# A fused state-space and MLP kernel with its whole order of operations replaced

## The chip, the cores and the metric

The kernel runs on one core of a Trainium2 chip. The metric is the device time in microseconds of one execution, the median of several runs.

## What is computed

A long convolution gated by two projections, and then a dense block, each behind a layer norm and with a residual; S = 2048 positions, D = 640 channels, F = 1728.

```python
x = A_q
h  = x + A(layernorm(x), A_k, A_v, shift_k, ssm_k, ssm_D)
h2 = h + B(layernorm(h), w1, b1, w2)

A(q, k, v): k_shift = sum over 4 taps of k shifted in time, times shift_k[:, tap]
            kv = k_shift * v
            y  = irfft(rfft(kv, 2S) * rfft(ssm_k, 2S))[:S] + kv * ssm_D
            return q * y
B(x):       h = x @ w1 + b1;  return (h * tanh(softplus(h))) @ w2
```

## The kernel before

Every piece of work is an operation with a name, the engines that may run it, and the operations it needs. A list written out in the source, `ORDER`, gives one total order of all operations. The emitting loop walks the list; every engine executes its own instructions in the order in which the list has them. A token may carry `@n`, which of the four PSUM pairs (1024 float32 columns per partition) the operation takes, and `:d`, `:a` or `:p`, which engine runs it if it is not the first that the operation allows. Loads and stores named `d_*`, the swaps `sw*` and the transposing copies `tr*` are issued by SyncE; three small loads, `d_dr`, `d_cst` and `d_sk`, are issued by ScalarE and stand in its instruction order between its other work.

The stages, with the names used below:

- **Constants.** `idn` and `kz` on GpSimd; `warm` loads ScalarE's table and runs one Mish; `wm` is nine matmuls on zeros on TensorE. `d_cst` loads the transform matrices that the s1 stages multiply with and a mask; `d_sk` loads the four taps per channel; `d_dr` loads the vector D.
- **The kernel of the convolution.** `d_n0` to `d_n4` load ssm_k; `dadd` adds D to its first sample; `k1pe` transposes it on TensorE, `k1ev` copies it out of PSUM; `s1kpe` / `s1kev` (20 groups) are the first step of the transform, `s2kpe` / `s2kev` (22 groups, with the tables `d_g0` to `d_g7`) the second. The swaps `sw` exchange its real and imaginary halves by DMA; they need every `s2kev`.
- **The taps.** `cfpe` is one matmul on the taps (it needs `d_cst` and `d_sk`), `coef` four copies on VectorE, and `wsh0` to `wsh3` spread them over a mask into tap matrices. The four `wsh` may run on GpSimd or VectorE; GpSimd is the first allowed.
- **k and v.** `d_k`, `d_v` load; `ktpe` transposes k on TensorE, `ktev` copies it out, `ktsh` copies a shifted row on GpSimd; `kspe` applies the tap matrices, `kv` multiplies with v on VectorE; `s1v` and `s2v` are the transform of kv.
- **Product and inverse.** `pr` (20 products on VectorE), `i1pe` / `i1ev` (20 groups), `i2pe`, `i2a`, `i2b` / `y` (16 tiles).
- **Norms and gate.** `d_x` loads q; `ln1`, `ln1p`, `lnx` are its layer norm on VectorE, GpSimd and ScalarE or GpSimd; `wb`, `h`, `bn`, `pow`, `hc` gate, add and normalise; `trpe` / `trev` or `tr` transpose the result.
- **The dense block.** `m1pe` multiplies with w1 (`d_w1`), `hb` applies Mish on ScalarE, `m2pe` multiplies with w2 (`d_w2a`, `d_w2b`, `d_w2c`; `w2z` zeroes two quarters), `res` adds the residual on VectorE, `d_out` stores. The 2048 rows are five units of 256, 256, 512, 512 and 512.

The copies out of PSUM go to ScalarE or VectorE, as the list says (`EV`). Helper lines: L264 is a copy on ScalarE, L266 on VectorE; L328 issues all plain loads of SyncE; L399 and L400 are the two halves of s1; L425 is stage 2, L453 a swap, L464 a product, L485 i1, L537 i2, L604 the first dense product, L669 and L677 the second.

Of the kernel before, what the change touches and what calls it, by code (L numbers as in the profile page):

```python
# [34 lines left out]
s2kev_108 s2kpe_72@3 kspe0_1@0 d_x1 s2kev_72 kv1_1 d_x0 s2kpe_66@2 s2kpe_102@3 s2kev_66 kv0_1 kspe4_1@1 s2kev_102 s2kpe_120@2 kv4_1 kspe3_1@0
s2kev_120 s2kpe_126@3 kv3_1 s2kpe_78@1 s2kev_126 s2kpe_0@2 s2kev_78 s2kpe_114@3 s2kev_0:d s2kpe_36@0 s2kev_114 s2kpe_54@1 s2kev_36:d s2kpe_84@2
s2kev_54 s2kpe_60@3 s2kev_84 ln1_0 kspe2_1@1 s2kev_60 s2kpe_48@0 kv2_1 ln1p0 s1vpe0_2@2 s2kev_48 s1vpe1_1@3 s1vev0_2:d s1vpe2_1@1 d_x2 s1vev1_1
s1vpe1_0@0 d_x3 s1vev2_1 s1vev1_0:d s1vpe4_3@2 s1vpe3_2@3 s1vev4_3 s1vpe0_0@1 s1vev3_2:d s1vpe2_2@0 s1vev0_0 s2kpe_90@2 s1vpe1_2@3 s1vev2_2 s2kev_90:d
s1vpe0_3@1 s1vev1_2 s1vpe1_3@0 s1vev0_3:d s1vpe0_1@2 s1vev1_3 s1vpe3_0@3 s1vev0_1:d s1vpe4_1@1 s1vev3_0 s2kpe_30@0 s1vev4_1:d s2v0pe_0@2 s2kev_30
s2v0pe_48@3 s2v0ev_0 ln1_1 sw1_0 s1vpe2_0@1 s2v0pe_64@0 sw1_1 s2v0ev_48 lnx0:p s1vev2_0:d s2v0pe_112@2 sw0_0 ln1p1 s2v0ev_64 sw4_0 s2v0pe_32@3  # L40
s2v0ev_112:d s2v0pe_80@1 sw3_1 s2v0ev_32 s1vpe3_1@0 lnx1:p sw0_1 ln1_2 s1vpe4_0@2 s2v0ev_80 sw3_0 s1vpe3_3@3 sw4_1 ln1_3 s1vev3_1 ln1p2 s1vpe2_3@1
sw2_0 s1vev4_0 s1vev3_3:d sw2_1 s1vpe4_2@0 lnx2:p s1vev4_2 s2v0pe_96@3 pr1_64 ln1p3 s2v0pe_16@2 s2v0ev_96 s2v2pe_32@0 s1vev2_3:d lnx3:p s2v0ev_16
s2v2pe_80@3 pr1_96 s2v2ev_32 s2v2pe_112@1 s2v2pe_64@2 s2v2ev_112 pr1_0 s2v2pe_48@0 s2v2ev_64 s2v2pe_0@1 pr0_96 s2v2ev_0 s2v2pe_16@2 pr1_32 s2v2ev_16
s2v1pe_96@1 pr0_64 s2v2ev_48 i1pe1_1@2 s2v2ev_80 s2v2pe_96@0 pr3_0 s2v1ev_96 i1pe1_2@3 pr3_32 i1ev1_1 s2v1pe_64@1 pr0_32 s2v2ev_96 s2v1pe_0@2 i1ev1_2
pr0_0 s2v1pe_32@0 s2v1ev_0 pr3_64 i1pe1_3@3 d_w14 s2v1ev_64 d_w10 i1pe0_2@2 pr3_96 d_w11 s2v1ev_32 d_w12 i1pe0_1@1 pr4_0 d_w13 i1ev1_3 d_t2m i1pe3_3@0
i1ev0_1 pr2_96 i1pe3_1@3 i1ev3_3 pr2_64 i1pe3_0@1 i1ev0_2 i1pe0_3@0 pr2_0 i1ev3_0 i1pe0_0@2 pr2_32 i1ev3_1 i1pe3_2@1 i1ev0_3 pr4_96 i1pe2_0@3 i1ev0_0
# [4 lines left out]
m1pe0_6@1 ln1_11 ln1p4 m1pe0_3@3 tr3 ln1p7 d_w2b ln1_13 h5 y8 lnx4:p m1pe0_2@0 hb0_6 ln1_9 ln1p8 wb4 lnx7:p hb0_3 wb7 lnx6 m1pe0_0@2 wb6 bn5 hb0_2 h4
hb0_0 h6 lnx8:p m1pe0_5@1 h7 ln1p15 ln1p11 m1pe1_1@3 bn4 m1pe1_4@0 lnx11:p pow5 wb8 hb0_5 m1pe1_2@2 ln1p9 hb1_1 m1pe1_0@1 hb1_4 wb11 bn7 hb1_2 hb1_0
ln1_14 ln1p10 m1pe1_5@3 m1pe1_3@0 hc5 m1pe1_6@2 i2pe9@1 hb1_5 hb1_3 pow7 bn6 i2pe14@3 pow6 h8 pow4 hc7 tr5 hb1_6 lnx15:p y9 m2pe0@0 bn8 y14 hc6
m2pe1@2 pow8 wb15 tr7 lnx9 hc4 wb9 ln1_12 lnx10 m2pe3@1 tr6 ln1p12 tr4 m2pe2@3 wb10 res3 res0 ln1p14 h11 h9 lnx14 res1 lnx12 bn9 h10 hc8 bn10 ln1p13
bn11 lnx13:p m1pe2_6@1 pow10 wb13 wb14 m1pe2_2@0 pow11 h13 hb2_2 hc10 wb12 h14 pow9 hc9 hc11 tr8 bn13 h12 bn14 m1pe2_3@2 tr10 hb2_6 m1pe2_4@0
m1pe2_0@1 d_out0 res2 bn12 pow13 h15 hb2_3 m1pe2_5@2 tr11 tr9 hb2_4 bn15 pow12 m1pe2_1@0 m1pe3_5@3 hb2_5 pow15 m1pe3_3@2 d_out1 hc13 hb2_0 m1pe3_2@1
hb3_5 hc15 hb3_2 m1pe3_0@3 pow14 tr13 hb3_0 m1pe3_6@1 hc12 hb3_6 hc14 m1pe3_1@3 m1pe3_4@1 hb2_1 hb3_4 d_out3 tr15 tr12 m2pe5@0 hb3_1 m2pe7@1 tr14
m2pe4@3 res7 res5 m2pe6@1 m1pe4_2@0 res4 m1pe4_5@3 res6 hb4_2 m1pe4_4@1 d_out2 d_out7 hb4_4 m1pe4_1@0 hb4_5 m1pe4_6@1 hb3_3 m1pe4_3@3 hb4_1 m2pe9@2
# [681 lines left out]
```

## Time and profile before

| | |
|---|---|
| median of 3 runs | 222.97 us (222.88 to 223.0) |
| the profiled execution | 223.02 us |
| its span, first to last instruction | 221.2 us |
| TensorE, matmul | 212.5 us busy |
| VectorE | 137.6 us |
| ScalarE | 127.9 us |
| GpSimd | 62.0 us |
| DMA | 30.98 MB moved |

All times inside the profile count from the first instruction. The 1.8 us between the span and the execution's time lie around it. A matmul's end is modelled, so TensorE's busy time is no measure of its load by itself. In the list of instructions a bracket gives the idle time of the engine just before, and what ended it; in a row of a stretch the columns are start and end, length, then busy time (and count) of TensorE's matmuls and weight loads, VectorE, ScalarE and GpSimd, the granted TensorE clock, the DMA engines' share and their GB/s.

### The profile page before, as it was taken

Reading aid. Unit: us, or ns where it says so; the run is one execution under the profiler, and the core shown is the slowest. Engines: PE = TensorE matmul, PEld = TensorE weight load, DVE = VectorE, ACT = ScalarE, POOL = GpSimd, SP = SyncE. Lnnn points to the kernel's source line nnn. Section 1 sums busy time; section 2 is a strip of 40 time slices with the busy share of each in tenths; the row PEclk is TensorE's granted clock in tenths of the full one; section 3 lists DMA queues with packets and bytes.
Section 4 is the critical chain, followed back from the end, with each engine's and each line's share of the span. In section 5 each row is a group of like instructions: output and inputs, shape, how many; then the busy total and the mean of one; then the engine's idle time right before and its main releaser. Section 6 shows DMA issues by size and latency. Waiting matters only on the chain.

```text
span 221.2 us, 6309 instructions
## 1 busy us (share of the span) xinstructions
PE 212.5 (96%) x2740; PEld 156.0 (71%) x2746; DVE 137.6 (62%) x236; ACT 127.9 (58%) x175; POOL 62.0 (28%) x123
## 2 busy tenths in 40 slices
...
DVE  2776899999999999899998679920002200002223
ACT  2389888999999999899753038426600257020000
...
DMA packets 19564, 30.98 MB, mean 140 GB/s; under 512 B 10705, under 2 KB 14929, under 8 KB 18769
## 3 DMA queue, kind: packets, MB, share of 16 engines
...
q10 hardware_dynamic: 336, 0.12, 0.2%
q14 instruction: 7, 0.05, 0.1%
q0 software_dynamic: 96, 0.00, 0.0%
...
## 4 chain that ended last, share of the span: by engine, by line
PE 72%; ACT 12%; DVE 6%; DMA 5%; issue 2%; SPq 1%; DVEq 0%; ACTq 0%
PE ps L669 26%; PE ps L604 26%; ACT uv L264 9%; PE ps L537 3%; DMA ks<-ks 3%; PE ps L399 3%; PE ps L425 3%; DMA ks<-in_A_ssm_k_dram 3%; PE ps L344 2%; PE ps L379 2%; DVE ks L266 2%; ACT ks L264 2%; PE ps L360 2%; DVE ra L365 1%; DVE uv L266 1%
## 5 line engine op out<-in xcount | busy, mean ns | idle before, releaser
L626 ACT ACTIVATE ks<-ps,b1s 128x512 bf16<-128x512 f32 (+1 forms) x69 | 36.2, 599 | 44.1 <-PE ps L604 35.1
L669 PE MATMUL ps<-ks 128*128 128x320 bf16 (+2 forms) x420 | 58.6, 299 | 0.0
L604 PE MATMUL ps<-G 128*128 128x512 bf16 (+1 forms) x319 | 57.2, 336 | 0.3
L669 PEld LDWEIGHTS <-ks 128*128 128x128 bf16 x420 | 40.6, 98 | 17.4 <-issue 1.3
L694 DVE TENSOR_TENSOR rb<-ps,rb 128x640 bf16<-128x640 f32 x15 | 11.8, 817 | 64.5 <-PE ps L677 52.2
L604 PEld LDWEIGHTS <-G 128*128 128x128 bf16 x325 | 31.4, 98 | 24.3 <-issue 1.1
L264 ACT CAST ks<-ps 128x960 bf16<-128x960 f32 (+3 forms) x48 | 39.3, 896 | 8.3 <-PE ps L400 5.0
L264 ACT CAST uv<-ps 128x1024 bf16<-128x1024 f32 x46 | 42.6, 1157 | 0.5 <-PE ps L485 0.4
L464 DVE TENSOR_TENSOR ks<-ks,uv 128x2048 bf16<-128x2048 bf16 x20 | 23.4, 1236 | 0.2 <-DMA ks<-ks 0.2
L425 PEld LDWEIGHTS <-G 128*128 128x128 bf16 x512 | 21.0, 96 | 3.1 <-issue 2.5
L485 PE MATMUL ps<-a_t,ks 128*128 128x128 bf16 (+1 forms) x416 | 17.1, 208 | 0.4
L485 PEld LDWEIGHTS <-ks 128*128 128x128 bf16 (+1 forms) x416 | 16.5, 114 | 1.0 <-issue 0.4
L266 DVE CAST uv<-ps 128x1024 bf16<-128x1024 f32 x14 | 16.4, 1210 | 0.2
L530 POOL TENSOR_SCALAR ra<-rb,r,nmr 128x640 bf16<-128x640 bf16 x11 | 12.5, 1133 | 9.9 <-PE ps L400 9.3
L425 PE MATMUL ps<-uv,G 128*128 128x64 bf16 (+1 forms) x384 | 12.9, 187 | 1.7 <-ACT uv L264 1.5
L550 DVE BATCH_NORM_STATS2 st<-rb 128x6 f32<-128x320 bf16 x32 | 14.0, 479 | 0.1
L516 DVE BATCH_NORM_STATS2 st<-rb 128x6 f32<-128x320 bf16 x32 | 13.7, 469 | 0.0
L365 DVE TENSOR_TENSOR ra<-ps,rb 128x1024 bf16<-128x1024 f32 x10 | 11.9, 1222 | 0.7 <-PE ps L361 0.5
L266 DVE CAST ks<-ps 128x1024 bf16<-128x1024 f32 (+2 forms) x10 | 11.3, 1160 | 1.0 <-PE ps L537 0.6
L528 ACT ACTIVATE ra<-rb,nmr,r 128x640 bf16<-128x640 bf16 x5 | 4.5, 925 | 11.9 <-POOL nmr L523 11.9
L425 PE MATMUL ps<-ks,G 128*128 128x160 bf16 x128 | 11.2, 230 | 0.1
L399 PE MATMUL ps<-cst,ra 128*64 128x128 bf16 x160 | 10.6, 219 | 0.7 <-ACT uv L264 0.5
...
## 6 DMA issues: line engine op xcount, KB each, us to landing
ks<-ks SPq DMA_DIRECT2D x10, 512.0 KB, 6.3
G<-tab_g SPq DMA_DIRECT2D x8, 512.0 KB, 11.1
ks<-in_A_ssm_k_dram SPq DMA_DIRECT2D x5, 512.0 KB, 6.5
ra<-in_A_k_dram SPq DMA_DIRECT2D x4, 640.0 KB, 10.6
rb<-in_A_v_dram SPq DMA_DIRECT2D x4, 640.0 KB, 11.4
...
```

What stands on the lines that cost most here:

```text
L264: nc.scalar.copy(o, i)
L266: nc.vector.tensor_copy(o, i)
L365: nc.vector.tensor_tensor(kv_w[:, m, :, 8 * h:8 * h + 8, :], p_.f32().rearrange("p (l t d) -> p d t l", l=4, t=8), raw_v[:, 8 * h:8 * h + ...
L399: nc.tensor.matmul(ps[0:64, dgl, :], lhs, mc, start=True, stop=True)
L425: nc.tensor.matmul(p_.f32()[:, o:o + n], g_v[:, f, :], src[:, :, f, :], start=True, stop=True)
L464: nc.vector.tensor_tensor(o, o, v, ALU.mult)
L485: nc.tensor.matmul(o, KS[r, k, b, :, l], a12[r, k, r], start=k == 0, stop=k == 1)
L516: nc.vector.bn_stats(st1[:, t, hh, :], xt(t)[:, hh * 320:(hh + 1) * 320])
L550: nc.vector.bn_stats(st2[:, t, hh, :], xt(t)[:, hh * 320:(hh + 1) * 320])
L604: nc.tensor.matmul(ph[:, o:o + w], w1[:, dc, fc * P:fc * P + P], lt[:, dc, 0:w], start=dc == 0, stop=dc == NDC - 1)
L626: nc.scalar.activation(hb[:, fc, 0:n], p_.f32()[:, i * 512:i * 512 + n], ACT.Mish, bias=b1s[:, fc:fc + 1], scale=1.0)
L669: nc.tensor.matmul(p_.f32()[:, o:o + n], lhs, w2[:, k, cols:cols + n], start=fc == 0, stop=single and fc == 13)
```

## The change

The list `ORDER` is replaced; nothing else. All operations stay, with their sizes. Changed are the order on every engine, the PSUM pair of many groups, the engine of some forty operations (33 of them copies out of PSUM before the last i1 copy, 16 from VectorE to ScalarE and 17 the other way; the five `dadd`; four `lnx`), and the order of the loads. The start of both lists and the place of the weights of the second product:

```diff
-d_dr wz idn d_n0 cz wm@0 small lane d_n1 d_cst d_sk d_n2 warm d_n3 d_n4 d_g0 dsel dcol dadd0 d_k2 k1pe0@1 d_k3 dadd1:p k1pe1@2 d_a12 k1ev0b d_k0 k1ev0
-s1kpe0_3@3 k1ev1 s1kpe0_1@0 s1kev0_3 d_k1 s1kpe0_0@1 dadd2 s1kev0_1 s1kpe1_3@2 s1kev0_0:d dadd3:p d_g4 s1kpe0_2@3 k1pe2@0 s1kev0_2 dadd4:p d_g1
-s1kev1_3 kz b1pe@1 k1pe4@3 k1ev2 c_b1 cfpe@2 k1pe3@1 k1ev4:a coef d_v0 s1kpe2_0@0 k1ev3 wsh1 s1kpe2_1@2 s1kev2_0 s1kpe4_3@3 d_g7 s1kev2_1:d s1kpe3_1@1
...
-ktpe0_3 ktpe0_2 s1kev1_2 ktpe2_0@3 ktpe2_3 ktpe2_2 d_v2 ktpe2_1 ktpe0_1 ktev2 ktpe1_0@1 ktev0:a ktpe1_1 ktpe1_3 ktpe1_2 s1kpe3_3@0 d_g5 ktev1 ktsh2
...
-y3 y6 pow1 wb2 i2pe15@3 i2pe7@0 pow0 hc1 d_w2a i2pe13@2 y15 wb3 hc0 y13 h2 i2pe10@1 bn2 y7 h3 bn3 pow2 pow3 d_w2c i2pe11@3 hc2 tr2 ln1_6 hc3 trpe1@2
...
+d_n0 d_n1 idn kz d_n2 d_dr wz d_n3 warm lane dsel small d_n4 dcol wm@0 dadd0:p d_g0 dadd1 k1pe0@1 dadd2:p d_cst k1pe1@2 k1ev0b k1ev0 s1kpe0_3@3 d_k2
+d_k3 s1kpe0_1@0 s1kev0_3 d_a12 s1kpe0_0@1 k1ev1 d_k0 s1kev0_0 s1kev0_1:d s1kpe1_3@2 dadd4 k1pe2@3 dadd3 cz k1pe4@0 s1kev1_3 d_k1 d_g7 b1pe@1 d_sk
+cfpe@2 c_b1 k1ev4:a k1ev2 k1pe3@3 coef k1ev3 s1kpe2_0@1 s1kpe2_2@2 s1kpe2_1@0 s1kpe1_2@3 d_g4 s1kev2_2:d s1kev2_0 s1kpe1_0@1 s1kpe4_3@2 s1kev2_1
+s1kev1_2:d d_v0 s1kev1_0 s1kpe3_2@0 s1kpe4_1@1 s1kpe0_2@3 wsh1 s1kev4_3 s1kev4_1 s1kev3_2:d s1kpe3_1@2 ktpe0_0@0 ktpe0_3 ktpe2_0@1 ktpe0_2 s1kev3_1:d
...
+s2kev_42 s2kev_30:d s1vev0_0 s1vpe1_0@3 s1vev3_2:d s1vpe2_2@0 s1vev1_0 s1vpe2_1@2 s1vpe1_1@1 s1vev2_1 sw4_0 s1vpe0_1@3 s1vev2_2:d s1vpe2_3@0 s1vev1_1
...
+s1vpe2_0@3 s1vev1_3 s1vpe3_3@0 s1vev2_0 s2v0pe_80@1 s1vev4_2:d ln1_2 s2v0pe_112@2 sw0_0 s1vev3_3:d sw1_1 s2v0ev_80 s2v0pe_64@3 s2v0pe_96@1 s2v0ev_64
+s2v0pe_16@0 s2v0ev_112:d pr0_64 s2v0ev_96 pr1_96 s2v0pe_0@3 ln1p0 s1vpe4_3@2 s2v0ev_0 d_x1 s2v0ev_16 s2v0pe_32@1 s2v0pe_48@3 s1vpe4_0@0 pr1_64 sw2_0
...
+ln1p7 tr2 h5 lnx7:p hb0_2 hb0_0 ln1_13 ln1_15 ln1p15 ln1_14 w2z hb0_5 bn5 tr3 m1pe0_3@0 m1pe0_1@2 ln1_8 hb0_3 hb0_1 m1pe1_2@1 hb1_2 m1pe1_4@3 lnx6 wb4
+wb6 m1pe1_1@0 ln1_11 d_w2a hb1_4 pow5 h4 h6 hc5 ln1_12 wb7 ln1p9 hb1_1 m1pe1_3@2 ln1p11 m1pe1_0@1 ln1p8 bn4 hb1_3 hb1_0 bn6 h7 pow6 pow4 m1pe1_5@3
...
```

Of the tap matrices, the list before has `wsh1`, `wsh3`, `wsh2` and `wsh0` without a mark, and so has the list after: they run on GpSimd in both.

More of the change, by code (lines that the diff above doesn't have):

```diff
@@ L35 @@
[L35 to L46, printed above, removed]
@@ L51 @@
[L51 to L58, printed above, removed]
@@ L59 @@
-d_out5 hb4_3 d_out6 m2pe8@0 m1pe4_0@3 hb4_6 m2pe11@1 hb4_0 res11 m2pe12@3 d_out4 m2pe14@1 res9 m2pe10@2 res12 m2pe13@3 res14 res13 d_out12 d_out14
-res10 m2pe15a@1 m2pe15b@3 d_out9 d_out13 d_out10 d_out11 res15a res8 d_out15a res15b d_out8 d_out15b
+d_n0 d_n1 idn kz d_n2 d_dr wz d_n3 warm lane dsel small d_n4 dcol wm@0 dadd0:p d_g0 dadd1 k1pe0@1 dadd2:p d_cst k1pe1@2 k1ev0b k1ev0 s1kpe0_3@3 d_k2
+d_k3 s1kpe0_1@0 s1kev0_3 d_a12 s1kpe0_0@1 k1ev1 d_k0 s1kev0_0 s1kev0_1:d s1kpe1_3@2 dadd4 k1pe2@3 dadd3 cz k1pe4@0 s1kev1_3 d_k1 d_g7 b1pe@1 d_sk
@@ new lines @@
+ktpe3_0@1 ktsh1 d_g2 d_g5 ktpe3_2 ktev4 ktpe3_1 ktpe3_3 s2kpe_126@0 s2kpe_72@3 kspe0_0@2 ktsh2 s2kev_126 ktev3 ktsh4 s2kpe_120@0 kv0_0 kspe1_0@1 kv1_0
+s2kev_72 d_v2 s2kpe_12@3 s2kpe_108@2 ktsh3 s2kev_120 kspe3_0@0 s2kev_12 s2kpe_24@1 kspe4_0@3 s2kev_108 s2kev_24 s2kpe_84@2 kv3_0 kv4_0 kspe2_0@0 d_v3
+s2kev_84 s2kpe_60@1 kspe0_1@3 kv2_0 s2kpe_18@2 s2kev_60 s2kpe_102@0 kspe3_1@1 kv0_1 s2kpe_36@3 kv3_1 s2kev_18 s2kev_102 kspe4_1@2 kv4_1 s2kpe_54@0
+s2kpe_114@1 s2kev_114:d s2kev_36 s2kev_54 d_x0 s2kpe_78@3 ln1_0 s2kev_78 s2kpe_96@2 s1vpe0_2@0 s2kpe_6@3 s2kev_96 s1vev0_2 s2kpe_48@1 kspe2_1@2
@@ new lines @@
+s2v0pe_16@0 s2v0ev_112:d pr0_64 s2v0ev_96 pr1_96 s2v0pe_0@3 ln1p0 s1vpe4_3@2 s2v0ev_0 d_x1 s2v0ev_16 s2v0pe_32@1 s2v0pe_48@3 s1vpe4_0@0 pr1_64 sw2_0
+pr1_0 s2v0ev_48 s2v1pe_0@3 s2v0ev_32 pr1_32 s1vev4_0 sw2_1 s1vpe4_1@1 s1vev4_3 s1vev4_1 lnx0:p pr0_0 pr0_96 s2v1pe_64@0 i1pe1_3@2 s2v1ev_0 sw3_1
+i1pe1_2@1 i1pe1_1@3 pr0_32 i1ev1_3 s2v1ev_64:d i1ev1_2 i1ev1_1 pr2_0 i1pe1_0@2 i1pe0_0@1 s2v2pe_80@0 sw3_0 s2v2pe_112@3 i1ev1_0 pr2_64 s2v2pe_64@2
+i1ev0_0 s2v2pe_96@1 s2v2ev_64 s2v2ev_96 s2v2pe_0@2 s2v2ev_80:d s2v2pe_32@0 s2v2pe_48@1 s2v2ev_0 s2v2ev_48 s2v2pe_16@2 s2v2ev_16 s2v2ev_112:d pr3_64
@@ new lines @@
+i1pe0_3@3 s2v2ev_32 i1pe0_1@1 i1pe0_2@2 i1ev0_1 i1ev0_2 s2v1pe_32@0 pr3_96 i1ev0_3 pr3_0 pr3_32 s2v1pe_96@1 i1pe3_1@2 s2v1ev_32 i1pe3_2@3 i1pe3_3@0
+s2v1ev_96 i1ev3_1 pr4_96 pr4_32 i1pe3_0@1 pr2_32 pr2_96 pr4_0 i1ev3_2 i1pe2_0@2 i1pe2_2@3 i1ev3_3 i1pe2_3@0 i1ev3_0 i1pe2_1@1 pr4_64 i1ev2_2:d d_w13
+i1ev2_0 i1pe4_3@2 i1ev2_3 i1ev4_3 ln1_1 d_t2m i1pe4_2@3 d_w10 i1ev4_2 i1pe4_1@0 i1ev2_1:d i1pe4_0@2 i1ev4_0 ln1p2 i2a1@1 i1ev4_1:d ln1p1 i2a2@3 lnx1:p
+i2b1 y1 lnx2:p i2a0@2 ln1_5 wb1 i2b0 y0 d_w14 i2pe12@0 d_x3 h1 lnx3:p wb0 bn1 ln1p5 i2b2 h0 i2pe5@1 pow1 bn0 i2a3@2 y2 y12 i2pe7@3 y5 i2pe4@0 wb2 y7
@@ new lines @@
+i2b3 i2pe8@1 hc1 d_x2 y3 d_w12 i2pe11@3 pow0 y4 i2pe6@2 trpe1@0 d_w11 h2 y8 lnx5:p y6 hc0 i2pe13@1 wb3 y11 trev1 bn2 trpe0@2 i2pe15@3 i2pe10@0 h3 bn3
+trev0:a pow2 pow3 y15 m1pe0_6@2 hc2 m1pe0_4@3 hc3 hb0_6 ln1_4 ln1p4 m1pe0_2@2 ln1_6 y13 hb0_4 y10 wb5 m1pe0_0@1 ln1p6 ln1_7 ln1_9 m1pe0_5@3 lnx4:p
+ln1p7 tr2 h5 lnx7:p hb0_2 hb0_0 ln1_13 ln1_15 ln1p15 ln1_14 w2z hb0_5 bn5 tr3 m1pe0_3@0 m1pe0_1@2 ln1_8 hb0_3 hb0_1 m1pe1_2@1 hb1_2 m1pe1_4@3 lnx6 wb4
+wb6 m1pe1_1@0 ln1_11 d_w2a hb1_4 pow5 h4 h6 hc5 ln1_12 wb7 ln1p9 hb1_1 m1pe1_3@2 ln1p11 m1pe1_0@1 ln1p8 bn4 hb1_3 hb1_0 bn6 h7 pow6 pow4 m1pe1_5@3
@@ new lines @@
+hb1_5 m1pe1_6@0 bn7 lnx8:p d_w2b d_w2c i2pe9@2 hb1_6 ln1p13 hc6 pow7 ln1_10 hc4 wb8 ln1p10 lnx13:p lnx9 tr5 tr4 i2pe14@1 lnx11 hc7 h8 m2pe0@3 wb11 bn8
+lnx15 ln1p14 m2pe1@0 y9 pow8 m2pe3@2 y14 h11 tr7 m2pe2@1 tr6 res3 bn11 m1pe2_4@2 wb9 res2 lnx14:p h9 hc8 m1pe2_3@1 bn9 lnx10:p d_out2 res0 wb10 hb2_3
+pow9 wb14 m1pe2_0@3 hc9 h14 h10 res1 bn14 d_out1 m1pe2_6@1 wb15 ln1p12 m1pe2_2@0 hb2_6 m1pe2_1@1 wb13 hb2_2 bn10 m1pe2_5@0 pow11 d_out0 tr9 pow10 hc11
+hb2_1 hb2_4 hc10 h13 lnx12 wb12 tr8 tr11 hb2_0 tr10 h12 m1pe3_6@1 bn12 h15 m1pe3_3@2 pow12 m1pe3_0@3 hb2_5 bn15 hb3_0 hb3_6 m1pe3_5@0 m2pe4@3 hb3_5
```

15 lines of the change are left out of this document (8 added, 7 removed).

## The prediction

> **What bounds the kernel now.** I read the page first, then the busy time by stretches, the waits of every engine and of the issuing queue, and the start of the run instruction by instruction.
>
> ```profile
> PE 212.5 (96%) x2740; PEld 156.0 (71%) x2746; DVE 137.6 (62%) x236; ACT 127.9 (58%) x175; POOL 62.0 (28%) x123
> DVE  2776899999999999899998679920002200002223
> ACT  2389888999999999899753038426600257020000
> ```
>
> VectorE and ScalarE are nearly full until about slice 20 of 40 and then empty out. TensorE's 96% is modelled and hides this, so the stretches decide:
>
> ```profile
> 20.00:30.00 10.00, 10.00 (x175) 9.55 (x175) 7.70 (x7) 8.31 (x9) 5.17 (x7) 1.00 1.02 411
> 30.00:40.00 10.00, 10.00 (x181) 9.89 (x179) 9.39 (x9) 8.53 (x10) 0.60 (x2) 1.00 0.69 241
> 40.00:50.00 10.00, 9.74 (x225) 8.73 (x223) 9.51 (x11) 9.92 (x12) 1.05 (x3) 1.00 0.48 161
> 70.00:80.00 10.00, 10.00 (x226) 9.86 (x224) 10.00 (x10) 10.00 (x13) 0.00 (x0) 1.00 0.61 210
> 130.00:160.00 30.00, 29.89 (x153) 14.13 (x152) 14.63 (x40) 14.97 (x26) 7.09 (x15) 1.00 0.29 67
> 160.00:190.00 30.00, 29.90 (x194) 17.63 (x195) 3.11 (x4) 8.74 (x15) 0.00 (x0) 1.00 0.07 23
> ```
>
> The columns after the length are PE, PEld, DVE, ACT, POOL, clock, DMA share, GB/s. In the tens from 40 and from 70 VectorE and ScalarE copy PSUM out and multiply almost without a pause (9.51 and 9.92, then 10.00 and 10.00); from 130 on TensorE multiplies without one (59.8 of 60). A reordering that keeps every operation can gain nothing inside those two parts. It can gain or lose where neither is full, which is before 30 us (7.70 and 8.31 of 10), and every microsecond lost there is carried through two full parts to the end.
>
> **The change at the start: where the tap load goes.** Before, ScalarE issues three small loads before any work: the D vector, `d_cst`, `d_sk`. After, `d_sk` stands on ScalarE behind three copies (s1kev0_3, s1kev0_0, s1kev1_3), and on TensorE `cfpe`, which needs it, stands ahead of `k1pe3` and all later s1k groups.
>
> ```profile
> 1.40 0.60 ACTq L272 DMA_DIRECT2D cst<-tab_cst  x1
> 2.03 0.45 ACTq L273 DMA_DIRECT2D sk_r<-in_A_shift_k_dram  x1
> 9.03 3.76 ACT L264 CAST ks<-ps 128x1024 bf16<-128x1024 f32 x4 [5.02 <-PE ps L400]
> 13.46 1.87 ACT L264 COPY ks<-ps 128x2048 bf16<-128x2048 bf16 x1 [0.59 <-PE ps L379]
> ```
>
> ```profile
> cst<-tab_cst ACTq DMA_DIRECT2D x1, 104.0 KB, 4.3
> sk_r<-in_A_shift_k_dram ACTq DMA_DIRECT2D x1, 5.0 KB, 4.9
> dful<-in_A_ssm_D_dram ACTq DMA_DIRECT2D x1, 5.0 KB, 2.2
> ```
>
> One copy is 3.76 / 4 = 0.94 us, so the third ends at 9.03 + 2.82 = 11.85. Can ScalarE issue the load then? The issuing queue shows a rule of this kernel: a load waits until the eighth load before it has landed.
>
> ```profile
> SPq L328 <- DMA G<-tab_g: 0.9, 1, 0.9
> SPq L328 <- DMA sk_r<-in_A_shift_k_dram: 0.7, 1, 0.7
> 6.99 0.33 SPq L328 DMA_DIRECT2D a_t<-tab_t2m  x1
> 12.68 0.33 SPq L328 DMA_DIRECT2D rb<-in_A_v_dram  x1
> 14.26 0.32 SPq L328 DMA_DIRECT2D G<-tab_g  x1
> ```
>
> sk_r was issued at 2.03 and landed at 2.03 + 4.9 = 6.93; the a_t load, eight loads later, starts at 6.99. The first v load starts at 12.68, having waited for G's first piece. After the change d_sk is the fifteenth load of ScalarE's and SyncE's common count, and eight before it stands that same G piece. So ScalarE issues it at 12.7, not at 2.03. For its transit I take 4.3, the row of cst: it too was alone at the head of ScalarE's queue with 512 KB loads on the other. The ends are 2.2 (dful, before there was traffic) and 4.9 (sk_r itself, behind cst). Landing L = 12.7 + 4.3 = 17.0, between 14.9 and 17.6.
>
> The Trainium skill, DMA: Bandwidth & Descriptors, section Queues, rings and completion order, says that each DMA engine serves its queues in turn packet by packet, so that a small load does not stand behind another queue's megabytes. By that rule alone it would land nearer 14.9; cst's 4.3 with the same traffic speaks against it.
>
> Who waits, from these rows:
>
> ```profile
> 10.21 0.22 PE L399 MATMUL ps<-cst,ks 128*64 128x128 bf16 x1
> 10.60 0.22 PE L399 MATMUL ps<-cst,ks 128*64 128x128 bf16 x1
> 11.01 1.16 PE ps L379 x16
> 13.35 0.20 PE L307 MATMUL ps<-sk_r,cst 32*128 32x80 bf16 x1
> 25.52 2.11 PE ps L344 x16
> 27.63 0.84 PE ps L425 x12
> 8.46 1.23 DVE L266 COPY ks<-ps 128x2048 bf16<-128x2048 bf16 x1 [0.39 <-PE ps L379]
> 13.60 1.01 DVE L312 CAST coef<-ps 32x80 bf16<-32x80 f32 x4
> 11.48 0.29 POOL L373 TENSOR_SCALAR ks<-ks,dcol 128x1 bf16<-128x1 bf16 x1 [1.00 <-DMA ks<-in_A_ssm_k_dram]
> ```
>
> A k1 block of transposes is 1.16, an s1k group of eight pairs 0.45 (10.21 to 10.60 and one step more), cfpe 0.20, coef 1.01, a transpose of k 2.11 / 16 = 0.13. TensorE goes k1pe2 (PSUM pair 3 is free at 9.97) 10.2 to 11.4, k1pe4 (the last piece of the kernel landed at 11.5) to 12.7, b1pe, and then stops at cfpe until L. VectorE ends k1ev2 at about 13.3 and waits for coef; ScalarE issues the load (0.45), ends c_b1 and k1ev4 (1.87) at about 15.2 and waits for s1kev2_0, whose group is ready at L + 0.20 + 1.16 + 0.45 = L + 1.8. Both copying engines stand idle for about 3.6 us.
>
> From L to the first s2k group: 1.85, then ScalarE's eleven remaining s1k copies, 11 x 0.94 = 10.3, between them about 1.6 in which TensorE makes 18 transposes of k (18 x 0.13 = 2.3) and nothing is ready to copy, and 0.45 for the last of the sixteen transposes that follow: L + 14.2. Before, that group starts at 27.63. So the change loses L - 13.4: with L = 17.0, 3.6 us; from 1.5 (L = 14.9) to 4.2 (L = 17.6). The tap matrices follow coef on GpSimd and are done in time:
>
> ```profile
> L320 POOL TENSOR_TENSOR rw<-cst,coef x4: 2062/2067/2072, 14.7 to 23.9; 128x1120 bf16<-128x1120 bf16 x4
> ```
>
> L + 1.2 + 4 x 2.07 = L + 9.5 and a short copy, against L + 14.2. Nothing hides the loss: from 30 us on the two copying engines have little left to give (9.39 and 8.53 of the ten from 30).
>
> **The rest, part by part.** *The dadd additions* change engines (0 and 2 to GpSimd, 1, 3, 4 to VectorE): under 0.3 us each, as in the row at 11.48; VectorE's 4 and 3 wait until 11.5 for the last kernel piece with k1ev2 behind them, which is in the 13.3 above. *d_cst* stands behind the table load, some 1.5 us later than 1.40 + 4.3 = 5.7; its first use follows k1ev0, which ends just before the copy at 8.46: 1.2 us of cover, nothing. *Copies between the engines*: sixteen move to ScalarE and seventeen to VectorE before the last i1 copy; after 27 us each engine keeps the same number (17 on VectorE), so the full part keeps its length. *The tap matrices* were on GpSimd in both orders; the title's last words change nothing.
>
> *The swaps* (KS halves) now start with the last s2k copy, before any s1v copy:
>
> ```profile
> 53.64 7.53 SPq L453 DMA_DIRECT2D ks<-ks  x7
> ks<-ks SPq DMA_DIRECT2D x10, 512.0 KB, 6.3
> ```
>
> They issue 1.08 apart and take 6.3; the first product, pr0_64, needs the fifth, 4 x 1.08 + 6.3 = 10.6 after the start. VectorE has eight copies and one LN statistic ahead of it, somewhat under 9 x 1.23 = 11.1. A wait of a few tenths on one of two engines: I put 0.2, between 0 and 0.5.
>
> *SyncE's other loads.* G's pieces and the v pieces trade places among themselves, the same bytes on the same queue; the v pieces for the second half come last and are used by the sixth kv product, late with the rest of the stage. d_x1 goes behind six swaps, d_x2 and d_x3 among the first weights; their statistics stand later on VectorE too. d_t2m is issued later against i2 but has one weight load ahead of it where it had five: nothing. *The second product's weights* (d_w2a) stood ahead of the transposes; now they stand behind tr2 and tr3:
>
> ```profile
> 99.24 2.63 SPq L579 DMA_TRANSPOSE G<-rw  x2
> ks<-in_B_w_dram SPq DMA_DIRECT2D x1, 2080.0 KB, 9.7
> 97.24 14.27 PE ps L604 x130
> 113.37 10.60 PE ps L669 x78
> ```
>
> 101.9 + 9.7 = 111.6 against the first use at 113.37: 1.8 us of cover, less the few tenths by which hc3 comes later. I put nothing; if the cover is gone, up to 1. In the last part unit 2's and unit 3's hc stand about as early on VectorE as before, and the last six products end in the same pair m2pe13, m2pe15b: nothing.
>
> Sum: the profiled execution took 223.02 (span 221.2 and 1.82 around it; the median shown is 222.97, the same). 223.0 + 3.6 + 0.2 = **226.8**.
>
> **The rivals.**
> *The tap load is early after all* (faster). If the count of eight does not hold for ScalarE and its queue runs ahead of copies that still wait, d_sk is issued well before 10.3 and lands before 12.7, when TensorE arrives. Then nothing stops and the order is tighter: 12.6 + 14.2 = 26.8 against 27.63, so 222.2. It decides at L = 13.4. The Trainium skill, Perfetto Trace Analysis, section Sequencer Loop, says that engine instructions go into a queue and wait there while the sequencer goes on, which is this rival. Against it:
>
> ```profile
> L320 POOLq EVENT_SEMAPHORE  x1: 17/17/17, 11.4 to 11.4; - x1
> ```
>
> GpSimd's queue took up this wait for cst, landed at 5.7, only at 11.4, when the addition ahead of it stopped waiting. Chance 0.13.
>
> *The load is quick*: 2.2 us as dful, L = 14.9, 224.7. Chance 0.20.
>
> *TensorE slows after its stop.*
>
> ```profile
> 1.24 4.02 PE L295 MATMUL ps<-rw 128*128 128x512 bf16 x9 [1.24 <-DVE rw L290]
> ```
>
> The first matmuls, of 512 columns, take 0.45 each; in the row at 97.24 256 columns take 0.11, twice the rate. A stop from 12.7 to 17.0 may bring the slow rate back: k1pe3 and the next four groups cost 1.2 + 4 x 0.45 more, half of it behind copies, so 1.5: 228.3. The Trainium skill, TensorE: Matmul & The Clock Gate, section Part 1: The HAM clock gate, has this for an idle window of about 3.4 us. No stop of that length follows the first matmuls in this trace, so no row tests it. Chance 0.12.
>
> *The load waits for a later one*: if the count is off by one or two and it waits for the k load that let the G piece go at 14.26, L is 18.6 to 19.2, 228.3 to 229.0. Chance 0.06.
>
> *The stop is swallowed*: the new order packs the copies until 88 us so much better that the end stays, 223.0. Against it: VectorE and ScalarE have hardly 4 us of pause between them there. Chance 0.07.
>
> **How the numbers follow.** 0.42 is left for my forecast, 226.8 (226 to 227.5). Faster by over 0.2% (0.45 us, about what a measurement of this kernel can tell from none): the first rival and a sliver of the last, 0.14. Within it: most of the last, 0.05. Slower: 0.81. The range goes from 223.4, which leaves out the first rival and half of the last, to 228.9.
>
> **What would show it.** In the profile after: the ACTq issue of sk_r near 12.7 and not near 2; TensorE's L307 near 17 with the longest wait of TensorE ahead of it, for that load; VectorE's coef near 17.2; the first L425 matmul on G and ks near 31; then the same full stretches, shifted; swaps' issue soon after the last s2k copy, the 2 MB load near 105 and L669 not waiting for it. Wrong: L307 before 13.5, or the shift gone by 88 us.

## The result and the profile after

The kernel after takes 232.88 us (median of 4 runs, 232.65 to 233.75), the kernel before 222.97 (222.88 to 223.0): 1.045 times as long, 95% interval 1.043 to 1.048. The prediction said 226.8, between 223.4 and 228.9. The sign was right; the loss of 9.9 us was forecast at 3.8.

The page of the kernel after, the lines that answer to those of before, and the granted clock by slice:

```profile
PE 214.9 (93%) x2746; PEld 157.8 (68%) x2746; DVE 139.0 (60%) x238; ACT 126.8 (55%) x174; POOL 58.9 (25%) x122
...
DVE  1738889999998789688999679624030300201032
ACT  2437678999996999597887102485322232052000
...
PEclk9988999999997999999999999999999999999999
```

VectorE now has notches at slices 14 and 17 of 40 and ScalarE at 13 and 17, inside the part that was to be full, and the clock dips at slices 3 and 4 and again at 13. The busy time by stretches of the kernel after (columns as before: length, PE, PEld, DVE, ACT, POOL, clock, DMA share, GB/s):

```profile
10.00:20.00 10.00, 6.76 (x124) 6.26 (x120) 5.15 (x11) 4.70 (x6) 2.96 (x2) 0.83 1.02 411
20.00:30.00 10.00, 9.94 (x226) 9.15 (x221) 8.56 (x8) 8.18 (x10) 6.84 (x6) 1.00 1.03 410
...
40.00:50.00 10.00, 9.59 (x162) 9.02 (x161) 9.41 (x13) 9.86 (x12) 0.70 (x2) 1.00 0.25 70
...
70.00:80.00 10.00, 9.31 (x188) 9.12 (x186) 8.00 (x8) 7.52 (x8) 0.00 (x0) 0.83 0.01 3
...
90.00:100.00 10.00, 7.58 (x230) 5.88 (x228) 7.35 (x13) 7.32 (x10) 4.63 (x9) 1.00 0.70 282
130.00:160.00 30.00, 30.00 (x177) 15.23 (x176) 19.44 (x49) 9.79 (x17) 14.42 (x32) 1.00 0.24 56
```

The tens from 70 were 10.00 and 10.00 on the two copying engines and are 8.00 and 7.52; the clock there is 0.83. From 130 on TensorE multiplies without a pause in both (29.89 and 30.00 of 30).

Four marks of the two profiled executions divide the 9.8 us by which the span grew (221.2 to 231.0). The first s2k copy starts at 31.91 instead of 28.13: **3.8 us**. The last i1 copy ends at 98.19 instead of 89.17; from the first mark that is 66.28 us instead of 61.04: **5.2 us** (5.3 in the expectations below). The first product of the dense part (L604) starts 8.8 us after it instead of 8.0: **0.8 us**. From there to the end it is 124 us in both.

**The start.** ScalarE's issue, the landing time, and who waited (timeline and issues of the kernel after):

```profile
10.23 0.35 ACTq L273 DMA_DIRECT2D sk_r<-in_A_shift_k_dram  x1
...
sk_r<-in_A_shift_k_dram ACTq DMA_DIRECT2D x1, 5.0 KB, 5.4
...
15.67 0.24 PE L307 MATMUL ps<-sk_r,cst 32*128 32x80 bf16 x1 [3.24 <-DMA sk_r<-in_A_shift_k_dram]
15.84 1.93 PE L379 MATMUL ps<-ident,ks 128*128 128x128 bf16 x16
...
15.95 1.00 DVE L312 CAST coef<-ps 32x80 bf16<-32x80 f32 x4 [3.29 <-PE ps L307]
...
18.81 5.61 ACT L264 CAST ks<-ps 128x1024 bf16<-128x1024 f32 x6 [4.40 <-PE ps L400]
```

The load is issued 0.3 before the third copy starts, takes 5.4, and TensorE, VectorE and ScalarE stop for 3.2, 3.3 and 4.4 us. The sixteen transposes behind it take 1.93 where 1.16 was normal: the granted clock is 0.5 from 15.30 to 18.71.

**The middle and the end of the full part.** TensorE's timeline of the kernel after, then the two copying engines':

```profile
67.25 0.83 PE L425 MATMUL ps<-uv,G 128*128 128x32 bf16 x27 [0.28 <-ACT uv L264]
69.39 0.29 PE L425 MATMUL ps<-uv,G 128*128 128x32 bf16 x5 [1.31 <-issue]
69.53 6.31 PE L485 MATMUL ps<-a_t,ks 128*128 128x128 bf16 x80
...
89.06 3.69 PE L485 MATMUL ps<-a_t,ks 128*128 128x128 bf16 x120 [0.30 <-DVE ks L464]
94.99 2.14 PE L485 MATMUL ps<-a_t,ks 64*128 64x64 bf16 x104 [2.24 <-issue]
```

```profile
76.35 2.36 DVE L266 CAST uv<-ps 128x1024 bf16<-128x1024 f32 x2 [2.00 <-PE ps L425]
82.05 9.21 DVE L464 TENSOR_TENSOR ks<-ks,uv 128x2048 bf16<-128x2048 bf16 x8 [1.08 <-ACT uv L264]
96.48 1.23 DVE L266 CAST uv<-ps 128x1024 bf16<-128x1024 f32 x1 [1.94 <-PE ps L485]
...
95.34 2.84 ACT L264 CAST uv<-ps 128x1024 bf16<-128x1024 f32 x3 [2.32 <-PE ps L485]
```

Twice TensorE stops where nothing in the profile holds it ("issue"), and both times in the middle of a group: after 27 of 32 matmuls at 68.08, and inside the last i1 groups at 92.75. Behind the first, the clock is 0.5 from 69.92 to 73.33. VectorE's pauses that follow, 2.00 + 1.08 + 1.94, add up to 5.0 us. Between the two marks VectorE is busy for 59.85 us (59.54 before) and idle for 6.4 us (1.5 before): nearly all of the 5.2 us is waiting, not work.

**What stops TensorE.** Its instructions come by DMA too:

```profile
q8 instruction: 21, 0.34, 0.6%
```

That is 21 packets of 16 KB for TensorE's 5,500 instructions: one per 256. In the records of instructions and packets one can count where TensorE stood when a packet started (matmuls, weight loads and the few instructions of its sequencer are counted together). In the quiet stretches of the dense part, packet j starts when TensorE begins about the 152nd to 164th instruction of block j (instruction 256 j + 150; call that due). The two late ones:

```
kernel after              due     started   ended    TensorE stopped    went on
packet 8                  61.72   67.02     68.00    after instr. 2497    69.39
packet 12                 86.97   92.67     93.65    after instr. 3521    94.99
```

2497 = 9 x 256 + 193 and 3521 = 13 x 256 + 193. Between the due point and the end of its supply TensorE has about 300 instructions; the packet needs 1.0 us, and TensorE goes on about 1.35 us after it has ended (1.2 to 1.6 us in all the stops listed further down). Ahead of packet 8 stood the swaps with a q load among them, ahead of packet 12 the weights. SyncE's issues of the kernel after:

```profile
51.34 5.97 SPq L453 DMA_DIRECT2D ks<-ks  x6
57.36 1.18 SPq L328 DMA_DIRECT2D rb<-in_A_q_dram  x1
58.58 4.13 SPq L453 DMA_DIRECT2D ks<-ks  x4
84.13 0.33 SPq L328 DMA_DIRECT2D G<-in_B_w_dram  x1
84.51 0.43 SPq L328 DMA_DIRECT2D ra<-tab_t2m  x1
84.98 0.90 SPq L328 DMA_DIRECT2D G<-in_B_w_dram  x2
85.93 0.97 SPq L328 DMA_DIRECT2D rb<-in_A_q_dram  x2
86.94 0.97 SPq L328 DMA_DIRECT2D G<-in_B_w_dram  x2
```

Packet 12 was due when seven of the last eight loads had been issued; it started behind the landing of the fourth (92.02). In the kernel before, the weights are issued from 72.95 on, because there the last readers of G (s2v1pe_32 and its neighbours) stand ahead of most i1 groups; after, s2v1pe_32 and s2v1pe_96 stand behind the first eight. In the kernel before, the packets due between 30 and 86 us wait 0.9 to 3.6 us and none comes too late; one waits 5.9 us at 88.6, but there TensorE multiplies long i2 columns and needs 18 us for its 300 instructions. The Trainium skill, Runtime: NRT & Kernel Launch, section Instruction fetch mechanics, has the blocks of 256 and calls the cost of a block's end mostly hidden. The trace agrees on the size; at the end of one block 2.24 us were not hidden here.

### The profile page after: what moved, and what is told of

Same layout as the page of the kernel before. It is cut to its first block, busy times and chain, and to the rows that moved or that the text cites. A ratio compares the mean times of both kernels' runs of the same rounds, so it can differ in the third digit from the quotient of the medians.

```text
span 231.0 us, 6313 instructions
## 1 busy us (share of the span) xinstructions
PE 214.9 (93%) x2746; PEld 157.8 (68%) x2746; DVE 139.0 (60%) x238; ACT 126.8 (55%) x174; POOL 58.9 (25%) x122
## 4 chain that ended last, share of the span: by engine, by line
PE 62%; ACT 6%; DVE 5%; issue 3%; POOL 0%; ACTq 0%; DVEq 0%; POOLq 0%
PE ps L669 25%; PE ps L604 25%; ACT uv L264 6%; PE ps L485 4%; DVE ks L464 3%; PE ps L425 2%; PE ps L611 1%; PE ps L677 1%; PE ps L537 1%; PE ps L400 1%; PE ps L399 1%; DVE st L550 1%; DVE rw L565 0%; DVE ks L544 0%; DVE rb L546 0%
## 5 line engine op out<-in xcount | busy, mean ns | idle before, releaser
L669 PE MATMUL ps<-ks 128*128 128x320 bf16 (+2 forms) x420 | 58.9, 299 | 0.0
L604 PE MATMUL ps<-G 128*128 128x512 bf16 (+1 forms) x325 | 58.1, 337 | 0.0
L669 PEld LDWEIGHTS <-ks 128*128 128x128 bf16 x420 | 40.8, 98 | 17.6 <-issue 0.8
L264 ACT CAST ks<-ps 128x960 bf16<-128x960 f32 (+3 forms) x49 | 39.9, 895 | 14.6 <-PE ps L400 12.0
L604 PEld LDWEIGHTS <-G 128*128 128x128 bf16 x325 | 31.1, 98 | 24.0 <-issue 1.7
L264 ACT CAST uv<-ps 128x1024 bf16<-128x1024 f32 x46 | 43.3, 1062 | 5.4 <-PE ps L485 4.5
L425 PEld LDWEIGHTS <-G 128*128 128x128 bf16 x512 | 20.6, 96 | 4.4 <-issue 3.8
L485 PE MATMUL ps<-a_t,ks 128*128 128x128 bf16 (+1 forms) x416 | 18.7, 215 | 2.6 <-issue 2.2
L485 PEld LDWEIGHTS <-ks 128*128 128x128 bf16 (+1 forms) x416 | 17.9, 117 | 3.0 <-issue 2.4
L521 POOL TENSOR_SCALAR ve<-mv 128x1 f32<-128x1 f32 x16 | 3.8, 241 | 51.7 <-DVE mv L517 51.0
L425 PE MATMUL ps<-uv,G 128*128 128x64 bf16 (+1 forms) x384 | 12.4, 187 | 3.2 <-ACT uv L264 1.9
L400 PE MATMUL ps<-cst,ra 128*64 128x128 bf16 x160 | 11.1, 221 | 0.6 <-issue 0.6
L399 PE MATMUL ps<-cst,ra 128*64 128x128 bf16 x160 | 11.0, 219 | 0.4 <-ACT ks L264 0.3
L530 POOL TENSOR_SCALAR ra<-rb,r,nmr 128x640 bf16<-128x640 bf16 x11 | 9.5, 869 | 7.1 <-issue 6.9
```

The source lines that it names most:

```text
L264: nc.scalar.copy(o, i)
L399: nc.tensor.matmul(ps[0:64, dgl, :], lhs, mc, start=True, stop=True)
L400: nc.tensor.matmul(ps[64:128, dgl, :], lhs, ms, start=True, stop=True)
L425: nc.tensor.matmul(p_.f32()[:, o:o + n], g_v[:, f, :], src[:, :, f, :], start=True, stop=True)
L485: nc.tensor.matmul(o, KS[r, k, b, :, l], a12[r, k, r], start=k == 0, stop=k == 1)
L604: nc.tensor.matmul(ph[:, o:o + w], w1[:, dc, fc * P:fc * P + P], lt[:, dc, 0:w], start=dc == 0, stop=dc == NDC - 1)
```

## The experiments

The theories: **starved** (TensorE runs out of instructions when a packet stands behind data, and a stop then lowers its clock), against **order** (the new order of TensorE's groups and of the copies makes the pauses by itself), and **carried** (only the late start counts, the rest follows from it). Times are medians; the kernel before took 222.87, 222.94 and 223.01 in the three series.

**e1_after_tap_first**

```
-  cfpe@2 ... behind:  b1pe@1 d_sk cfpe@2
+  d_dr d_sk wz d_n3 warm ...
```

> The kernel after, with the tap load back at the head of ScalarE's queue; nothing else is changed. If the whole loss of the start comes from that load, TensorE no longer stops at L307 (no wait of 3.2 us for sk_r), the granted clock stays at 1.00 between 10 and 20 us, the first s2k copy comes near 27.3 instead of 31.9, and with the rest as in the kernel after the time is 232.9 - 4.6 = 228.3 us. If the loss of the middle (5.3 us between the first s2k copy and the last i1 copy) is only a consequence of the late start, it goes as well and the time is near 223. If the start is bound by something else, the time stays over 231.

227.76 us, 5.1 less than the kernel after. The stop at L307 is gone, the clock is 1.00 from 10 to 20, and the first s2k copy starts at 27.87. But the stops of the middle came back in other places: "issue" stops after instructions 1985 (1.43 us), 2241 (2.39) and 3521 (0.78), a clock of 0.5 from 61.51 to 64.93. So carried is wrong: the middle loses by itself.

**e2_before_tap_late**

```
-  d_dr wz idn ... d_cst d_sk d_n2
+  ... s1kev0_1 d_sk s1kpe1_3
```

> The kernel before, with the tap load behind ScalarE's second copy (s1kev0_1), so that it is issued near 10 us as in the kernel after; nothing else is changed. It measures the first step of the prediction by itself. If a late start is carried to the end one for one: a stop of TensorE at L307 of about 3.2 us, a granted clock of 0.5 for one stretch of 3.4 us after it, first s2k copy near 31.9 instead of 28.1, and 223.0 + 3.8 = 226.8 us. If the slack of the later parts takes it up: 223 to 224.5. If the late start brings the later stops of TensorE with it (near 68 and 93 us in the kernel after): over 229.

225.12 us, 1.011 of before (1.008 to 1.013): 2.2 us, between the first and the second case. The load was issued at 9.09 and TensorE stopped for 1.7 us, not 3.2; no slow stretch followed. The first s2k copy came 1.35 later, the last i1 copy 1.48, with no later stop of TensorE; the profiled run took 224.5, 1.6 over before. So the old order carried this late start to the end about one for one, without running dry.

**e3_after_x1_behind_swaps**

```
-  s2v0ev_0 d_x1 s2v0ev_16
+  i1ev2_2:d d_x1 d_w13
```

> The kernel after, with the q load d_x1 behind the last swap on SyncE instead of between the sixth and the seventh; nothing else is changed. In the kernel after, TensorE stops in the middle of a group at 68.08 for 1.31 us, after its 2497th instruction, while the 16 KB instruction packet that it needs started 5.3 us after the others' rule (150 instructions into the block before) would have it, behind the swaps and this load. If the stop is a lack of instructions behind data, 640 KB less ahead of the packet (1.6 us) let it land near 66.4: no hole at 68, no stretch of clock 0.5 from 69.9 on, VectorE's pauses of 2.00 and 1.09 mostly gone, 232.9 - 3 = 229.8 us. If VectorE waits because the i1 groups stand ahead of s2v2pe_80 on TensorE, the pauses stay and the time is 231.5 to 233.

233.01 us (231.18 to 234.07): nothing gained. The stop at 2497 went, but stops after 1985 (1.37), 2241 (1.03) and 3521 (3.01) were there, each with 193 left over 256. Without the q load among them the ten swaps are still traffic enough; with it, another packet came too late. That the load decides no more than this rests on one trace of each kernel.

**e4_after_w1_behind_i1**

```
-  deps=all_s2) for i in range(NDC)]
+  deps=all_s2 + i1_pes) for i in range(NDC)]     (and d_t2m ahead of d_w1*)
```

> The kernel after, with the five loads of the first weights (2.1 MB) waiting for the last i1 group of TensorE instead of starting at 84; nothing else is changed. In the kernel after, TensorE stops in the middle of the i1 groups at 92.74 for 2.24 us, after its 3521st instruction, while the instruction packet starts 5.7 us late behind these loads. If that is the cause, the packet lands before 91, the hole goes, the last i1 copy ends near 96 instead of 98.2, and the time is 232.9 - 2.2 = 230.7 us (less if the weights then come late for m1 at 107). If i1pe4 waits for the last product or for a buffer, the hole stays and the time is 232.9.

233.43 us (231.65 to 236.9). The added dependence orders the list only and made no wait; SyncE issued the weights at 83.45 as ever, and d_t2m moved to 64.56. Packet 12 waited 6.1 us and TensorE stopped after 3521 for 2.71. The run says nothing on weights held back; it says that 1 MB less of 4.4 is not enough.

**e5_after_w1_gated**

```
+  g_w1 = OP("g_w1", "sp", emit=lambda e: nc.sync.dma_start(gs[0:1, 8:16], uv[0:1, 8288:8296]))
   ... d_t2m i1pe4_2@3 g_w1 d_w10 ...
```

> The kernel after with one 16-byte copy more on SyncE, behind the second load of the stretch from 84 on (d_t2m): it reads what i1ev2_3 writes, so that SyncE holds the other six loads (3.1 MB) until about 92. If TensorE stopped at 92.74 because its instruction packet stood behind these loads, the packet (due at 87.0) now starts by 90 and not at 92.7, the stop of 2.24 us in the i1 groups goes, and the time is 232.9 - 2.2 = 230.7 us. If the stop has another cause (the product, a PSUM buffer), it stays and the time is 232.9 or more.

231.55 us. SyncE and TensorE of this run:

```profile
83.77 0.43 SPq L328 DMA_DIRECT2D ra<-tab_t2m  x1
92.30 0.80 SPq L494 DMA_DIRECT2D gs<-uv  x1
...
88.31 5.88 PE L485 MATMUL ps<-a_t,ks 128*128 128x128 bf16 x224 [0.30 <-DVE ks L464]
```

The packet started at 89.4 instead of 92.7, all 224 matmuls run in one stretch, and the last i1 copy ends at 95.25 instead of 98.19. Starved holds for this stop. Of the 2.9 us, 1.9 reached the end of this execution (230.90 against 232.81), because the weights came late: the dense part's first products waited 0.8 us for them. In the medians 1.3 is left. The stop at 2497 (1.20) is there as in the kernel after.

**e6_after_swaps_gated**

```
+  g_sw = OP("g_sw", "sp", emit=lambda e: nc.sync.dma_start(gs[0:1, 0:8], ks[0:1, 256:264]))
   ... s2v0ev_0 g_sw d_x1 ...
```

> The kernel after with one 16-byte copy more on SyncE, behind the sixth swap: it reads what the first product pr0_64 writes, so that SyncE holds d_x1 and the last four swaps until about 62.7 instead of 57.4. The instruction packet due at 61.7 then finds nothing of them ahead of it. If the lack of instructions made the stop at 68.08 (1.31 us) and the stop the stretch of clock 0.5 from 69.9 to 73.3, both go, and with them most of VectorE's pauses of 2.00 and 1.09: 232.9 - 3 = 229.9 us. If the order of TensorE's groups makes the pauses, they stay: 232 to 233.

232.34 us, 0.5 less instead of 3, and not clear of the spread of its runs (230.9 to 233.1). The stop at 2497 and the slow stretch from 70 on are gone, and the last product ends 1.1 earlier than in the kernel after although the start was 1.7 later. But this execution had a slow stretch of 6.8 us at the start, and its stop at 3521 (2.60) was followed by one of 3.4 us from 93.68. The stop that the gate was meant for is gone; that the rest of the gain was lost to the others is read from this one trace.

**e7_tap_first_both_gated**: e1, e5 and e6 together.

> The kernel after with the tap load at the head (as in the run before, 227.8) and both gates on SyncE. In that run TensorE lacked instructions at 53.5 (1.43 us), at 59.2 (2.39 us) and at 89.3 (0.78 us), and one stretch of 3.4 us at clock 0.5 followed the second. If these stops are the rest of the loss, the second, the third and the slow stretch go or shrink: 227.8 - 2.4 - 0.8 - 0.8 = 223.8 us, between 222.5 and 225. If the new order loses by itself in the middle (who copies what, i1 ahead of s2v2), it stays at 226 to 228.

225.22 us, 1.010 of before (1.008 to 1.013), just above the range expected. By stretches:

```profile
50.00:60.00 10.00, 9.26 (x283) 8.34 (x278) 9.96 (x12) 9.96 (x12) 1.92 (x4) 1.00 0.65 263
60.00:70.00 10.00, 9.23 (x230) 8.88 (x226) 10.00 (x10) 9.88 (x12) 0.00 (x0) 1.00 0.75 279
70.00:80.00 10.00, 9.22 (x239) 8.93 (x236) 9.72 (x10) 10.00 (x12) 0.00 (x0) 1.00 0.19 54
```

TensorE's matmuls have no stop for "issue" over 0.3 us, there is no slow stretch before the end, and the last i1 copy ends at 88.85, 0.3 earlier than in the kernel before. The new order of copies, groups and swaps costs nothing there: order is wrong.

**e8_after_kept_warm**

```
+  for _ in range(28):
+      nc.tensor.matmul(wk_p.f32()[:, 0:256], wz[:, 0:P], wz[:, P:P + 256], start=True, stop=True)
   ... b1pe@1 d_sk wk@2 cfpe@2 ...
```

> The kernel after with 28 matmuls more of 256 columns on zeros (about 56 instructions, 3.1 us) on TensorE right ahead of cfpe, where it stands still for the tap load; their result is not used. Two things are told apart. The clock: without an idle stretch it stays at 1.00 between 10 and 20 us, the work of the 3.4 us behind the stop takes half as long, the first s2k copy comes near 30.4 instead of 31.9, and the time falls by up to 1.5 to 231.4; if the slow stretch was hidden behind the copies, nothing changes. The lack of instructions: if blocks of 256 set where TensorE stops, it stops again after counts that leave 193 when divided by 256 (2497, 3521 of all its instructions), which are now 56 instructions earlier in its program; if a place of the program makes the stop, the counts are 2553 and 3577.

233.41 us. TensorE's timeline and waits (the lines below L300 stand 7 further down in this kernel):

```profile
12.40 3.23 PE L302 MATMUL ps<-rw 128*128 128x256 bf16 x28
15.97 0.19 PE L314 MATMUL ps<-sk_r,cst 32*128 32x80 bf16 x1 [0.34 <-DMA sk_r<-in_A_shift_k_dram]
16.10 1.22 PE L386 MATMUL ps<-ident,ks 128*128 128x128 bf16 x16
...
PE ps L492 <- issue: 3.9, 1, 3.9
```

The clock stays at 1.00, the transposes take 1.22 instead of 1.93, and the first s2k copy comes 15.3 us after the tap product instead of 16.2: the slow clock cost 0.9 of the 3.8. The gain was lost again: TensorE stopped for 3.9 us in the i1 groups. Where it stopped is the better result: after 2497 and after 3777 of its instructions. 3777 is 14 x 256 + 193. With 56 instructions more ahead of it, 2497 is another place of the program than in the kernel after; the program's places would be 2553 and 3577. A wait of 0.87 us for a copy, after 2799 in the kernel after, did move with the program, to 2855.

**f1_new_front_old_rest**

```
   ORDER: after with d_sk at the head, g_sw, g_w1 at i1ev3_0, weights ahead of q, up to i1ev4_0;
          then before, from i2a0 on
```

> A version that may beat both: the order after up to the last i1 copy, with the tap load at the head and the two gates on SyncE (the second one at i1ev3_0, some 2 us earlier than in the run before, and the five weight pieces ahead of the q pieces), then the order before from i2 on. In the run with both gates the last i1 copy ended at 88.85, 0.3 earlier than in the kernel before, but the first product of the dense part began 1.5 us later than there. If the order of the i2 part made that, the time is 222.9 - 0.3 = 222.6 us, between 222.2 and 223.2. If the i1 results come in an order that does not suit the old i2 part, or the late weights made it, 224 or more.

223.88 us (222.98 to 226.62), 1.0025 of before (1.0009 to 1.0042), between the two cases expected: no version beats the kernel before. In the profiled run the last i1 copy ends at 88.75 and the first dense product starts at 96.93, 8.2 us later; both are ahead of before (89.17 and 97.16), but the median is not; why was not traced.

**f2_before_w1_late**

```
+  g_w1 = OP("g_w1", "sp", emit=lambda e: nc.sync.dma_start(gs[0:1, 8:16], ks[0:1, 16384:16392]))
   ... pr4_0 g_w1 d_w14 d_w10 d_w11 d_w12 d_w13 d_t2m ...
```

> The kernel before with one change that has nothing to do with the new order: the five weight loads and d_t2m (3.2 MB) are held on SyncE, by a 16-byte copy that reads what the product pr4_0 writes, from 73 to about 77.5, so that they are issued right ahead of an instruction packet (due at 80.4) and of the i1 groups. If a lack of instructions behind data is what costs the kernel after its time, it can be made in this kernel too: the packet starts over 4 us late, TensorE stops for 1 to 3 us after its 3265th instruction (12 times 256 and 193) in the i1 groups, and the time is 224.5 to 227 us. If the i1 groups have slack or packets are not held by data, 223.0.

224.12 us, 1.007 of before (1.0045 to 1.0094): slower, by just less than the range expected. SyncE and TensorE:

```profile
77.39 2.25 SPq L328 DMA_DIRECT2D G<-in_B_w_dram  x5
...
81.83 4.34 PE L485 MATMUL ps<-a_t,ks 128*128 128x128 bf16 x124
87.68 2.52 PE L485 MATMUL ps<-a_t,ks 64*128 64x64 bf16 x103 [1.51 <-issue]
```

Packet 12 started 5.05 us late and TensorE stopped for 1.5 us after instruction 3521, with a clock of 0.5 from 88.47 on. (The 3265 expected was a slip of one block: packet 12 carries the instructions behind 13 x 256 + 193.) So the same stop can be made in the old order by the time of its loads alone. What it costs depends on the clock: three of the five runs have a mean granted clock of 1.00 and take 223.93 to 224.12 us, two have 0.992 (in the traced one a single stretch of 3.41 us at half clock) and take 225.42 and 225.56.

**f3_gates_weights_earlier**: e7 with g_w1 at i1ev3_0 and the order d_w10 d_w14 d_w12 d_w11 d_x3 d_x2.

> The run with the tap load at the head and both gates (225.2), with the second gate some 2 us earlier (at i1ev3_0) and the weight pieces ahead of the q pieces. There the first product of the dense part waited 0.43 us for a weight piece. If the lateness of the weights is what is left of the loss, the time falls by 0.4 to 1.0, to 224.5; if the order of the i2 part makes it, it stays over 224.8.

224.12 us, 1.1 less than e7, as expected if the late weights were the cause (the runs, 223.52 to 225.01 here and 224.66 to 225.98 there, overlap a little). The last i1 copy ended at 88.28 and the first dense product started at 97.42, 9.1 later, where f1 with the old i2 order took 8.2. So the new i2 order costs about 0.9 there; in the medians only 0.2 of it shows (224.12 against 223.88).

**f4_after_both_gated**: both gates, the tap load late.

> The kernel after with both gates on SyncE and the tap load where the kernel after has it. One gate alone gave 231.55 and the other 232.34. If each removes one stop of TensorE and what follows is carried to the end, both together leave the loss of the start alone: 225.2 + 3.8 = 229.0 us. If the stops replace one another (another packet comes late), over 231.

230.46 us, between the two cases expected: 5.2 more than e7, where 3.8 was to be the loss of the start. The first s2k copy is 4.4 later than in e7; and other packets now come late: stops after 1985 (1.04) and 2753 (0.98), again 193 over 256. From the first s2k copy to the last i1 copy this run takes 62.2 us, 4.1 less than the kernel after, and e7 takes 60.7, 4.7 less than e1 (65.4): with the tap load late or early, holding the traffic back takes away most of the 5.2 us.

All stops of TensorE without a wait, as gaps between instruction starts of 0.6 us and more:

```
                           stops after TensorE instruction (us)
before, e2                 none
after                      1985 (0.60)  2497 (1.48)  3521 (2.44)
e1 tap first               1985 (1.43)  2241 (2.39)  3521 (0.78)
e3 x1 behind swaps         1985 (1.37)  2241 (1.03)  3521 (3.01)
e4 t2m early               1985 (0.66)  2497 (1.20)  3521 (2.71)
e5 w1 gated                2497 (1.20)
e6 swaps gated             2241 (0.75)  3521 (2.60)
e7, f1, f3                 none
e8 kept warm, 56 more      2497 (1.23)  3777 (4.12)
f2 before, w1 late         3521 (1.70)
f4 gated, tap late         1985 (1.04)  2753 (0.98)
```

Every number leaves 193 when divided by 256.

## Why the prediction was right and wrong

**The tap load: right in kind, and right in size at its first mark by luck, since two errors offset each other.** I let it wait for the G piece that is eight loads earlier, until 12.7. The count of eight holds, but the load's turn came two places earlier than I counted it: it waited for the third piece of the SSM kernel, landed at 8.44, so the third copy's wait decided (its group ended on TensorE at 10.19), and it went at 10.23. The transit was 5.4, not 4.3. It landed at 15.6, inside my bounds of 14.9 to 17.6. From there to TensorE's first s2k group I counted 14.2; it was 15.9 (31.52); of the 1.7 more, 0.9 was the clock (e8), and the rest was not traced. Together 3.8 at the first s2k copy, against the 3.6 forecast. To the end the term was too small: by the medians the late load costs 5.1 (e1).

**The clock rival came true, beside the forecast and not in its place.** I priced it at 1.5 and gave it 0.12; it cost 0.9 at the start and came a second time at 69.92, where I had seen no stop. The early-load rival was wrong in its own terms: the issue did run ahead of the copy (by 0.3 us), but only once that copy's wait was met.

**The step that failed is "the full part keeps its length": it grew by 5.2 us.** I argued from the copying engines' counts alone: 17 copies on VectorE in both orders, and 10.00 of 10.00 busy. Their work did stay the same (VectorE 59.85 us against 59.54), and with the traffic held back the part keeps its length (60.7 us in e7). What I did not price were TensorE's own instructions. I saw that the swaps start with the last s2k copy and priced only the wait of the first product (0.2; the trace shows none). I put d_t2m's later place at nothing, and the prediction says nothing of s2 and i1 groups changing places, which lets the first weights go at 84.13 instead of 72.95. Both changes put megabytes ahead of an instruction packet just where TensorE uses 300 instructions in 5 to 6 us. That makes most of the 5.2 us: e5, e7 and f4 take these stops away by moving the traffic, f2 makes one in the old order, and e8 shows that the count of instructions, not the place in the program, sets where TensorE stops.

**The i2 order** is no term of the sum and cost 0.8 (0.9 between f3 and f1). *The second product's weights* were put at nothing: right, as the kernel after shows:

```profile
106.95 14.36 PE L604 MATMUL ps<-G 128*128 128x256 bf16 x130
...
123.00 3.29 PE L669 MATMUL ps<-ks 128*128 128x320 bf16 x23
```

No wait stands ahead of L669; the 2 MB load landed at 121.81. *The dense part* kept its 124 us.

**What the medians divide.** From 223.0: the new order with its traffic held back and the tap load early is at 224.1 (f3), without the gates at 227.8 (e1), with the late tap load at 232.9. So the packets behind data cost up to 3.6, the late tap load 5.1, and the rest 1.1. The 3.6 holds the better place of the weights in f3; the gates of e7 alone gain 2.5 on e1, and those of f4 2.4 on the kernel after, but they make the weights late. The 5.1 is 5.2 with the gates (f4 against e7). The tap load costs 2.2 in the old order (e2) and 5.1 in the new one: there it is issued later and TensorE has less to do ahead of it (a stop of 3.2 against 1.7, and the clock), and it moves the packets against the swaps. By the marks of the traces, 4.0 us of the 5.1 lie ahead of the first s2k copy (31.91 against 27.87) and 0.85 between it and the last i1 copy (66.28 against 65.43); how much of these is the last point was not separated.
